# Top-32 attention and an MLP-mixer on one core: when casts, weights and the first transpositions are issued, and a new table of priorities

## The chip, the cores and the metric

The kernel runs on one core of one Trainium2 chip. Its engines run at the same time, each through its own list of instructions in order: TensorE (PE in the profile: matmuls and transpositions), VectorE (DVE), ScalarE (ACT), GpSimd (POOL) and SyncE (SP, which here only issues DMAs). The metric is device microseconds of one launch; the time before is the median of three runs, 937.52 us (936.66 to 938.66).

## The reference

Inputs are q, k and v of shape (8 batches, 8 heads, 576 rows, 64 columns) in float32, and four weights. For each batch and head:

```
scores = (q @ k.T) / 8                      # 576 x 576
kth    = 32nd largest score of each row
p      = exp(scores - rowmax) where scores >= kth, else 0
attn   = (p / sum(p)) @ v                   # 576 x 64
```

The heads of a batch are laid side by side as x (576 x 512), and the mixer computes

```
u   = x + (relu(x.T @ w_tok1) @ w_tok2).T   # w_tok1 576x256, w_tok2 256x576
out = u + relu(u @ w_ch1) @ w_ch2           # w_ch1 512x1536, w_ch2 1536x512
```

The output is (8, 576, 512) in float32.

## The kernel before, in words

**Pairs.** The unit of work is a pair of heads of one batch: 32 pairs (`u` = 0 to 31), four to a batch. Each pair's rows make nine tiles of 128 rows by 576 scores, in two groups: group 0 has four tiles, group 1 five. One pair goes through these steps:

1. SyncE loads q and k of the pair (`load_one`, L276: three DMAs each, the third for the 64 last rows; lines L289 and L292), and v from a bfloat16 copy in DRAM, `v16`. That copy is made a batch at a time by casting DMAs that GpSimd issues (`vconv`, L297). The buffers for q, k, the scores of each group and the transposed q and k are double.
2. TensorE transposes q and k (`qk_tr` L303, `qk_tail_tr` L319) and ScalarE copies the results out of PSUM (L317, L330).
3. TensorE computes the scores (`s1_mm` L337, `s0_mm` L360, `st_mm` L379), ScalarE copies them to SBUF (L350, L370, L390). Three PSUM banks, `s0`, hold scores.
4. For each group VectorE finds each row's 32nd largest score. `upper` (L401) takes the larger of the two halves of each row; `split4` (L428, L432) halves further; four rounds of MAX8 and MATCH_REPLACE8 (L445, L448) draw the largest values from these lists. Meanwhile GpSimd makes the list of the smaller halves (`both_bits` L408, `lower_bits` L416: "the list pass"), which VectorE reads in `low_round` (L461); `combine` (L466) gives the bound.
5. ScalarE makes the exponentials (L508). Five of nine tiles ("turned") are masked before that by ScalarE (`steep`, L526) and GpSimd (`sink`, L534, after `raise_kth`, L520) and then transposed by a DMA that SyncE issues (`turn`, L539). The other four are masked by ScalarE (`below_act`, L550), and transposed on TensorE (L556, L559) with ScalarE copying out (L579).
6. TensorE multiplies by v (`o_mm`, L624), VectorE inverts the denominators (`o_den`, L636), ScalarE scales (`o_ev`, L646); then the token half of the mixer for these 128 channels (`h1_mm` L666, `ut_mm` L687).

After a batch's fourth pair comes the channel half: `h2_mm` (L717, ScalarE L730) and `out_mm` (L746, ScalarE L754). For the last batch this is split: partial sums over three quarters of the channels (`pre_mm`, L1039) are made while pair 31 is in work, and `rest_mm`, `join`, `begin` and `accum` (L1103, L1115, L1081, L1094) close it.

**What sets the order.** The program is not written in the order in which it runs. Each step is added to a `Plan` as a task with an engine, an assumed duration, a priority, the tasks that it depends on and the buffers that it takes and frees. `Plan.order` (L58) then walks through assumed time: whenever an engine is free, it takes, among the tasks whose dependencies have ended and whose buffers are free, the one of the smallest priority. The result is one fixed list per engine, which on the chip runs in order, each instruction waiting for what it needs. A priority is 100 times the pair's number plus a constant of the kind of step, from the table `RANK` (L18): so a difference of 100 between two kinds is one pair. The smallest goes first. In the planner's idle time of TensorE `spare` (L261) puts in matmuls that compute nothing that is used.

Two of the planner's due times matter below. A DMA is a task without an engine (`DQ`), with a slack: a load of v waits until 12 us of assumed time after the cast of its batch is issued. And q's and k's transposition is assumed to be ready 1.3 us after the load was issued and SyncE's lag of 1.2 us.

**At the start** GpSimd issues, after the constants, in priority order: w_tok1 and w_tok2 (30), the cast of v of batch 0 (40), that of batch 1 (100 * 4 - 350 = 50), w_ch1 in two halves (210, 211), w_ch2 in two halves (220, 221), and the casts of batches 2 to 7 (450 and on). A cast depends on nothing but the cast before it.

Of the kernel before, what the change touches and what calls it, by code (L numbers as in the profile page):

```python
# [17 lines left out]
RANK = {  # L18
    "pre_mm": 21, "pre_ev": 49, "rest_mm": -29, "begin": 196, "flags": 11, "rush": 10, "rush6": -93, "load": -300,
    "qk_tr": -163, "qk_ev": -49, "s_mm": -158, "s_ev": -434, "st_mm": -106, "st_ev": -297, "keep": -185, "exp_u": 105,  # L20
    "steep": 63, "sink": 111, "exp_t": 88, "below": 404, "p_tr": -318, "p_ev": -292, "pt_tr": 92, "pt_ev": 68,
    "o_mm": 134, "o_ev": -231, "h1_mm": -373, "h1_ev": -445, "ut_mm": -358, "ut_ev": 1, "out_mm": 272, "out_ev": 225,
    "h2_mm": -3, "h2_ev": 1,
}
# [116 lines left out]
def kernel(  # L141
# [11 lines left out]
    nc = tc.nc  # L153
# [16 lines left out]
    SP = NS * P  # L170
# [12 lines left out]
    NPAIR = H // 2  # L183
# [92 lines left out]
    def load_one(st, name, src, b, p):  # L276
        if name == "v":
            src = v16
            st["vb"] = take("vb", vbufs)
            t = st["vb"][:, :, :, 0:D]  # L280
# [7 lines left out]
        for hh in range(2):  # L288
            nc.sync.dma_start(  # L289
                out=t[:, 0:NT, hh, :], in_=rws[hh, 0:W, :].rearrange("(t p) c -> p t c", p=P)  # L290
            )
        nc.sync.dma_start(  # L292
# [479 lines left out]
    add = pl.add  # L772

    def plan_weights():
        tasks = {}

        def piece(names, moves, prio):
# [9 lines left out]
            a = add("POOL", 1.2 * len(moves), prio, ld)  # L787
            x = add("DQ", 0.0, 0, lambda: None, deps=[a], slack=10.0)
# [20 lines left out]
    conv = {}  # L809
    wt = plan_weights()  # L810
    later = []
    chain = {}
# [3 lines left out]
    def plan_unit(u):  # L816
# [6 lines left out]
        if p == 0:  # L823
            conv[b] = add("POOL", 1.0, U - 350 if b else 40, lambda: vconv(b), deps=[conv.get(b - 1)])
            conv[b, "in"] = add("DQ", 0.0, 0, lambda: None, deps=[conv[b]], slack=12.0)
        for name, src in (("q", q), ("k", k), ("v", v)):
            ld[name] = add("SP", 1.75, U + RANK["load"], lambda name=name, src=src: load_one(st, name, src, b, p),
                           deps=[conv[b, "in"]] if name == "v" else [],
                           acq=[("vb" if name == "v" else "ld" + name, u)])
        vc = add("DQ", 0.0, 0, lambda: None, deps=[ld["v"]], slack=1.3)  # L830
        ev, prev = [], None
        for i in range(2):
            a = add("PE", 0.61, U + RANK["qk_tr"], lambda i=i: qk_tr(st, i), deps=[ld["qk"[i]], prev], acq=[("tp", u, "q", i)] + ([] if i else [("qkT", u)]), slack=1.3)
# [15 lines left out]
        for g in range(2):  # L849
# [35 lines left out]
            nms[g] = chain["bits"] = lob  # L885
# [395 lines left out]
```

## Time and profile before

| | |
|---|---|
| median of 3 runs | 937.52 us (936.66 to 938.66) |
| profiled execution, device time | 937.98 us |
| its span, first to last instruction | 936.1 us |
| granted TensorE clock, mean | 0.978 |
| PE, DVE, ACT, POOL busy | 856.1, 855.4, 843.7, 667.2 us |

The profiled execution lasted 1.9 us longer than its span, and is 0.46 us above the median. PE's busy time holds the spare matmuls too.

How to read it: the views give microseconds from the first instruction. A row of the timeline has the start, the duration, the engine, the line of the kernel, the operation, the tiles written and read, and how many instructions were merged; in brackets stands how long the engine had been idle before, and what ended that. "SPq" is SyncE's queue, whose rows are DMA issues; "PEld" is TensorE's weight load. In a table of windows each engine has its busy time in that stretch and, in brackets, its instructions. "q0" is the queue of GpSimd's DMAs, "q1" that of the DMAs that SyncE issues.

### The profile page before, as it was taken

How to read it: one execution, taken by the hardware profiler on the slowest of the kernel's cores; microseconds unless marked ns; L12 is line 12 of the kernel's file. 1: busy time of each engine (PE TensorE's matmuls, PEld its weight loads, DVE VectorE, ACT ScalarE, POOL GpSimd, SP SyncE). 2: the span in 40 equal slices, each digit the busy share in tenths (PEclk: the TensorE clock that was granted, in tenths of full speed). 3: DMA queues.
4: the chain of work that ended last, by engine and by line, in shares of the span. 5: the costliest groups of instructions: out<-in, count | busy, mean ns of one | idle time of the engine just before them, and what ended most of it. 6: DMA issues, size and time to landing. Idle time of an engine off the chain costs nothing.

```text
span 936.1 us, 22100 instructions
## 1 busy us (share of the span) xinstructions
PE 856.1 (91%) x7095; PEld 470.6 (50%) x7204; DVE 855.4 (91%) x3983; ACT 843.7 (90%) x1994; POOL 667.2 (71%) x510
## 2 busy tenths in 40 slices
PE   3479999999999999999999999999999999999895
PEld 3244555555554555545554555555554555555542
DVE  1495999999999999999999999999999999999942
ACT  1248999999999999999999999999999999999862
POOL 4258588777877778777787777877788778778700
PEclk8779999999999999999999999999999999999998
DMA  9962322233333334324332324323332334222201
GB/s 176 212 128 55 65 62 61 42 71 81 82 61 68 68 82 91 68 40 91 76 72 61 80 77 91 61 43 87 80 71 58 79 82 66 32 43 70 52 3 54
DMA packets 230124, 68.90 MB, mean 74 GB/s; under 512 B 222256, under 2 KB 224624, under 8 KB 229744
## 3 DMA queue, kind: packets, MB, share of 16 engines
q1 hardware_dynamic: 226624, 58.96, 29.8%
q0 software_dynamic: 3376, 8.46, 4.7%
q8 instruction: 58, 0.95, 0.4%
q14 instruction: 66, 0.54, 0.2%
HBM read 40.50 MB, written 14.16 MB: 58 GB/s over the span
## 4 chain that ended last, share of the span: by engine, by line
ACT 42%; PE 29%; DVE 19%; DMA 4%; issue 3%; SPq 3%; ACTq 0%; another core or an unknown queue 0%; DVEq 0%
ACT SS L370 6%; DVE A L445 6%; PE s L360 6%; ACT pb L508 5%; ACT U L550 5%; DVE hx L448 5%; ACT xb L646 4%; ACT E L508 4%; ACT U L526 4%; PE mps L717 4%; DMA qL<-in_q_dram 3%; ACT pt L579 3%; PE mps L265 3%; ACT H2T L730 3%; PE mps L746 2%
## 5 line engine op out<-in xcount | busy, mean ns | idle before, releaser
L408 POOL TENSOR_TENSOR lo<-SS 128x1152 int32<-128x1152 int32 x64 | 168.6, 2634 | 161.6 <-DVE A L445 134.1
L445 DVE MAX8 A<-hx 128x8 f32<-128x72 f32 (+2 forms) x1152 | 263.9, 293 | 0.0
L534 POOL TENSOR_TENSOR SS<-SS,U 128x576 f32<-128x576 f32 x158 | 198.5, 1283 | 10.8 <-ACT U L526 10.8
L448 DVE MATCH_REPLACE8 hx<-A,hx 128x72 f32<-128x72 f32 (+1 forms) x864 | 199.4, 242 | 0.0
L416 POOL TENSOR_TENSOR lo<-lo,hi 128x1152 int32<-128x1152 int32 x64 | 168.7, 2636 | 0.0
L360 PE MATMUL s<-qkT 64*128 64x512 f32 x512 | 156.2, 653 | 0.0
L370 ACT COPY SS<-s 128x512 f32<-128x512 f32 x256 | 141.6, 620 | 14.9 <-PE s L360 14.7
L401 DVE TENSOR_TENSOR hi<-SS 128x1152 f32<-128x1152 f32 x64 | 99.7, 1558 | 32.6 <-ACT SS L370 32.6
L508 ACT ACTIVATE pb<-SS,nmax 128x576 bf16<-128x576 f32 x158 | 124.9, 812 | 2.8 <-POOL SS L534 2.7
L526 ACT ACTIVATE U<-SS,kbig 128x576 bf16<-128x576 f32 x158 | 124.7, 813 | 0.9 <-POOL kbig L520 0.9
L520 POOL TENSOR_SCALAR kbig<-A 128x4 f32<-128x4 f32 (+1 forms) x63 | 101.5, 1611 | 30.1 <-DVE A L466 27.7
L461 DVE MAX8 A<-lo 128x8 f32<-128x288 f32 x256 | 100.1, 442 | 5.9 <-POOL lo L416 5.9
L717 PE MATMUL mps<-UT,wc1b 128*128 128x64 bf16 (+1 forms) x645 | 99.2, 282 | 6.4 <-ACT H2T L730 4.3
L556 PE MATMUL tp<-identB,E 128*128 128x128 bf16 (+1 forms) x650 | 101.4, 222 | 3.9 <-ACT pt L579 2.2
L559 PE MATMUL tp<-identN,U 128*128 128x128 bf16 (+1 forms) x650 | 95.8, 220 | 9.9 <-ACT U L550 8.7
L746 PE MATMUL mps<-wc2b,H2T 128*128 128x512 bf16 (+1 forms) x412 | 102.2, 380 | 1.3 <-issue 1.3
L508 ACT ACTIVATE E<-SS,nmax 128x576 bf16<-128x576 f32 x130 | 100.4, 805 | 0.2 <-POOL nmax L494 0.2
L550 ACT ACTIVATE U<-SS,A 128x576 bf16<-128x576 f32 x125 | 99.8, 821 | 0.0
L265 PEld LDWEIGHTS <-identB 128*128 128x128 bf16 x726 | 60.8, 101 | 59.1 <-issue 8.1
L717 PEld LDWEIGHTS <-wc1b 128*128 128x128 bf16 x672 | 46.4, 97 | 71.9 <-issue 37.4
L556 PEld LDWEIGHTS <-E 128*128 128x128 bf16 (+1 forms) x650 | 63.7, 100 | 35.7 <-issue 23.2
L559 PEld LDWEIGHTS <-U 128*128 128x128 bf16 (+1 forms) x650 | 62.9, 100 | 35.1 <-ACT U L550 27.1
(113 smaller groups left out, 1612.2 us busy)
## 6 DMA issues: line engine op xcount, KB each, us to landing
qL<-in_q_dram SPq DMA_DIRECT2D x64, 128.0 KB, 2.5
kL<-in_k_dram SPq DMA_DIRECT2D x64, 128.0 KB, 2.6
out_dram<-ob SPq DMA_DIRECT2D x28, 256.0 KB, 2.3
v<-in_v_dram POOLq DMA_DIRECT2D x8, 576.0 KB, 28.8
vb<-v SPq DMA_DIRECT2D x64, 64.0 KB, 2.3
pt<-pb SPq DMA_TRANSPOSE x158, 2.4
wc1b<-in_moe_w_ch_dram POOLq DMA_DIRECT2D x2, 768.0 KB, 16.8
wc2b<-in_moe_w_ch_dram POOLq DMA_DIRECT2D x2, 768.0 KB, 25.3
```

The lines of the kernel that those rows point to most:

```text
L360: nc.tensor.matmul(out=x[:, :], lhsT=T[rows[hh], 0, t * P : (t + 1) * P], rhs=T[rows[hh], 1, 0:W], start=True, stop=True,)
L370: nc.scalar.copy(out=st["SS", t // 2][:, 2 * (t % 2) + hh, 0:W], in_=st["s0", t][hh][:, :])
L408: nc.gpsimd.tensor_tensor(out=x[:, 0:4, :].bitcast(i32), in0=SS[:, 0:4, 0:HALF].bitcast(i32), in1=SS[:, 0:4, HALF:S].bitcast(i32), op=ALU.add,
L416: nc.gpsimd.tensor_tensor(out=x, in0=x, in1=st["hi"][:, 0:4, :].bitcast(i32), op=ALU.subtract)
L445: nc.vector.max(A[:, i, at], hx[:, i, 0:w])
L448: nc.vector.match_replace(hx[:, i, 0:w], A[:, i, TOP[r] : TOP[r] + 8], hx[:, i, 0:w], NEG)
L508: nc.scalar.activation(out=x, in_=srow(st, i), func=AF.Exp, bias=st["nmax", g][:, a : a + 1], scale=scale,)
L526: nc.scalar.activation(out=U[:, :], in_=srow(st, i), func=AF.Relu, bias=st["kbig", g][:, a : a + 1], scale=-STEEP,)
L534: nc.gpsimd.tensor_tensor(out=x, in0=x, in1=st["U", i][:, :], op=ALU.subtract)
L556: nc.tensor.matmul(out=out, lhsT=st["E", i][:, cols], rhs=identB[:, :], start=True, stop=False)
L559: nc.tensor.matmul(out=out, lhsT=st["U", i][:, cols], rhs=identN[:, :], start=False, stop=True)
L717: nc.tensor.matmul(out=ps[:, 0 : hi - lo], lhsT=wc1b[:, cc, fc * P : (fc + 1) * P], rhs=mst["UT"][:, cc, lo:hi], start=(cc == 0), stop=(cc ...
```

## The change

Five things are done; the values of the first are all in the diff.

- `RANK`, the table of priorities, has new values for all 34 kinds. They reach from -2256 to +2324, where they reached from -445 to +404.
- The cast of a batch's v (`conv`) depends now, for batches 1 to 7, on GpSimd's list pass of group 0 of the second pair of the batch before (`lobs[u - 3, 0]`). Its assumed slack is 18 us instead of 12.
- The cast of batch 0 and the weights are held (`held`): the cast of batch 0 and w_tok1 with w_tok2 until the list pass of pair 0's group 0, both halves of w_ch1 until that of its group 1, and one half of w_ch2 each until those of pair 1's two groups.
- k of pair 0 is loaded by ScalarE's queue instead of SyncE's.
- The transpositions of q and k of pairs 1, 2 and 3 depend now on the last score matmul of the pair before (`chain["first"]`).

```diff
 RANK = {
-    "pre_mm": 21, "pre_ev": 49, "rest_mm": -29, "begin": 196, "flags": 11, "rush": 10, "rush6": -93, "load": -300,
-    "qk_tr": -163, "qk_ev": -49, "s_mm": -158, "s_ev": -434, "st_mm": -106, "st_ev": -297, "keep": -185, "exp_u": 105,
-    "steep": 63, "sink": 111, "exp_t": 88, "below": 404, "p_tr": -318, "p_ev": -292, "pt_tr": 92, "pt_ev": 68,
-    "o_mm": 134, "o_ev": -231, "h1_mm": -373, "h1_ev": -445, "ut_mm": -358, "ut_ev": 1, "out_mm": 272, "out_ev": 225,
-    "h2_mm": -3, "h2_ev": 1,
+    "pre_mm": -619, "pre_ev": -763, "rest_mm": 23, "begin": 2294, "flags": 2033, "rush": -1060, "rush6": -1432, "load": -1622,
+    "qk_tr": 925, "qk_ev": 319, "s_mm": -2256, "s_ev": 861, "st_mm": -827, "st_ev": -1306, "keep": -1462, "exp_u": -1655,
+    "steep": -1178, "sink": 343, "exp_t": 592, "below": 2324, "p_tr": -1113, "p_ev": 1133, "pt_tr": 284, "pt_ev": 680,
+    "o_mm": -541, "o_ev": -678, "h1_mm": -281, "h1_ev": -760, "ut_mm": -245, "ut_ev": -1638, "out_mm": 1654, "out_ev": 724,
+    "h2_mm": 2300, "h2_ev": -1055,
 }
...
-    def load_one(st, name, src, b, p):
+    def load_one(st, name, src, b, p, queue=None):
+        queue = queue or nc.sync
...
-            nc.sync.dma_start(
+            queue.dma_start(
...
             a = add("POOL", 1.2 * len(moves), prio, ld)
+            held.append(a)
...
+    held = []
     wt = plan_weights()
+    lobs = {}
...
-            conv[b] = add("POOL", 1.0, U - 350 if b else 40, lambda: vconv(b), deps=[conv.get(b - 1)])
-            conv[b, "in"] = add("DQ", 0.0, 0, lambda: None, deps=[conv[b]], slack=12.0)
+            conv[b] = add("POOL", 1.0, U - 350 if b else 40, lambda: vconv(b), deps=[conv.get(b - 1), lobs.get((u - NPAIR + 1, 0))])
+            if b == 0:
+                held.insert(0, conv[b])
+            conv[b, "in"] = add("DQ", 0.0, 0, lambda: None, deps=[conv[b]], slack=18.0)
         for name, src in (("q", q), ("k", k), ("v", v)):
-            ld[name] = add("SP", 1.75, U + RANK["load"], lambda name=name, src=src: load_one(st, name, src, b, p),
+            aside = u == 0 and name == "k"
+            ld[name] = add("ACT" if aside else "SP", 1.75, U + RANK["load"],
+                           lambda name=name, src=src, aside=aside: load_one(st, name, src, b, p, nc.scalar if aside else None),
...
-            a = add("PE", 0.61, U + RANK["qk_tr"], lambda i=i: qk_tr(st, i), deps=[ld["qk"[i]], prev], acq=[("tp", u, "q", i)] + ([] if i else [("qkT", u)]), slack=1.3)
+            a = add("PE", 0.61, U + RANK["qk_tr"], lambda i=i: qk_tr(st, i), deps=[ld["qk"[i]], prev] + chain.get("first", []), acq=[("tp", u, "q", i)] + ([] if i else [("qkT", u)]), slack=1.3)
...
-            nms[g] = chain["bits"] = lob
+            nms[g] = chain["bits"] = lobs[u, g] = lob
+            if u < 2:
+                for t in held[: 2 if u == 0 else 1]:
+                    pl.after(t, lob)
+                    held.remove(t)
+            chain["first"] = smm[-1:] if u < 3 else []
```

More of the change, by code (lines that the diff above doesn't have):

```diff
@@ L288, in load_one @@
         for hh in range(2):
-            nc.sync.dma_start(
+            queue.dma_start(
                 out=t[:, 0:NT, hh, :], in_=rws[hh, 0:W, :].rearrange("(t p) c -> p t c", p=P)
             )
-        nc.sync.dma_start(
+        queue.dma_start(
             out=t[0:TAIL, NT, :, :], in_=rws[:, W:S, :].rearrange("h p c -> p h c")
```

## The prediction

> **What bounds the kernel now.** I read the page first, then a table of windows cut where VectorE's first pass over a pair's lists begins, then the timeline of the first 42 us and of the stretch from 62 to 99 us. The page: three engines are busy for about 90% of the span, so shares alone say nothing. The row of q0 is GpSimd's DMA queue, the last two rows are what the change moves.
>
> ```profile
> span 936.1 us, 22100 instructions
> PE 856.1 (91%) x7095; PEld 470.6 (50%) x7204; DVE 855.4 (91%) x3983; ACT 843.7 (90%) x1994; POOL 667.2 (71%) x510
> ...
> q0 software_dynamic: 3376, 8.46, 4.7%
> ...
> v<-in_v_dram POOLq DMA_DIRECT2D x8, 576.0 KB, 28.8
> wc1b<-in_moe_w_ch_dram POOLq DMA_DIRECT2D x2, 768.0 KB, 16.8
> ```
>
> The windows are: up to VectorE's first list pass, pair 0, pair 1, pairs 2 to 4, 5 to 23, 24 to 30, VectorE's part of pair 31, and the end.
>
> ```profile
> core 0: us, PE busy (x) PEld busy (x) DVE busy (x) ACT busy (x) POOL busy (x), PEclk, DMA share, GB/s
> 0.00:36.30 36.30, 16.07 (x132) 12.08 (x132) 2.70 (x9) 6.37 (x13) 11.64 (x33) 0.72 1.04 187
> 36.30:62.20 25.90, 13.63 (x91) 7.88 (x90) 25.83 (x122) 8.32 (x22) 15.43 (x8) 0.74 0.84 174
> 62.20:99.30 37.10, 35.43 (x256) 17.87 (x261) 26.77 (x125) 30.99 (x63) 22.85 (x18) 1.00 0.25 57
> 99.30:177.80 78.50, 74.89 (x608) 40.78 (x617) 78.40 (x371) 73.22 (x167) 60.53 (x45) 1.00 0.33 64
> 177.80:672.80 495.00, 474.88 (x4008) 261.55 (x4070) 494.62 (x2338) 492.06 (x1181) 383.27 (x285) 1.00 0.34 72
> 672.80:857.10 184.30, 176.62 (x1468) 96.38 (x1490) 182.18 (x862) 182.79 (x439) 149.91 (x105) 1.00 0.30 60
> 857.10:886.10 29.00, 26.02 (x260) 15.82 (x262) 26.52 (x128) 26.20 (x62) 23.10 (x15) 1.00 0.22 62
> 886.10:930.00 43.90, 38.55 (x283) 18.27 (x288) 18.37 (x41) 23.70 (x55) 0.43 (x1) 1.00 0.12 35
> ```
>
> From pair 2 on VectorE is the bound: pairs 5 to 23 take 495.0 us, 26.05 each, and it works 494.62 of them. ScalarE stands right behind it with 492.06. What is not bound work is at the start (VectorE works 2.70 of 36.3 us), in pair 1 (26.77 of 37.10, so 10.3 idle) and in the end of 43.9 us, where TensorE is busy for 38.55.
>
> **Part 1, the start.** The order on TensorE and what it waited for:
>
> ```profile
> 3.83 5.51 PE L265 MATMUL O<-identB 128*128 128x128 bf16 x60 [3.83 <-DVE O L255]
> ...
> 9.18 0.61 PE L307 MATMUL tp<-identF,qL 128*128 128x128 f32 x4
> ...
> 9.62 1.06 PE L265 MATMUL O<-identB 128*128 128x128 bf16 x16
> ...
> 10.52 0.61 PE L307 MATMUL tp<-identF,kL 128*128 128x128 f32 x4
> ...
> 11.97 0.66 PE L337 MATMUL s<-qkT 64*128 64x64 f32 x8
> ...
> 23.23 1.09 PE L307 MATMUL tp<-identF,qL 128*128 128x128 f32 x4 [10.60 <-DMA qL<-in_q_dram]
> ...
> 32.10 1.09 PE L307 MATMUL tp<-identF,kL 128*128 128x128 f32 x4 [5.78 <-DMA kL<-in_k_dram]
> ...
> 33.12 2.08 PE L360 MATMUL s<-qkT 64*128 64x512 f32 x4
> ...
> 35.23 1.07 ACT L370 COPY SS<-s 128x512 f32<-128x512 f32 x2 [1.42 <-PE s L360]
> ...
> 35.67 0.85 PE L337 MATMUL s<-qkT 64*128 64x64 f32 x8
> ...
> 36.34 1.36 DVE L401 TENSOR_TENSOR hi<-SS 128x1152 f32<-128x1152 f32 x1 [32.56 <-ACT SS L370]
> ...
> 39.55 1.07 ACT L370 COPY SS<-s 128x512 f32<-128x512 f32 x2 [0.54 <-PE s L360]
> ```
>
> Pair 0 is transposed by about 11.1 us and its first scores are made at 11.97. Then pair 1's q stands next in TensorE's list and has not landed: 10.60 us of waiting; after half of pair 0's scores comes pair 1's k: 5.78 more. So VectorE starts at 36.34. The loads are late because all casts and weights were issued ahead of them or among them; the row of SyncE's loads (L289) shows the best, the median and the worst time to land:
>
> ```profile
> DMA to landing us min/median/max: 2.0/2.5/30.2
> ```
>
> The change takes both causes away: with pair 1's transpositions behind pair 0's last scores, TensorE's list can't meet a late load in between, whatever the DMAs do. The new start step by step. q of pair 0 keeps its 60 spare matmuls, since its assumed due time (1.75 + 1.2 + 1.3 = 4.25 us) is unchanged: 9.18. k is now assumed ready at 1.75 + 0.15 + 1.3 = 3.2, before q's transposition has ended, so the 16 spares between them go: 10.52 - (9.18 + 0.61) = 0.73 us earlier, first scores at 11.24. From there to the last score copy of a group costs what it cost for group 1 of this pair: 35.67 to 39.55 + 1.07 = 40.62, so 4.95, and 0.04 to VectorE: 16.2. That is **20.1 us** earlier. The dearer price would be two halves as at 33.12 to 35.23 + 1.07, 3.18 each, behind 0.66: 7.0, a start at 18.3 and 18.0 us. I take 4.95, the same steps with no late load among them. Three DMA issues on ScalarE's queue cost nothing: it has nothing to copy before q is transposed at 9.18.
>
> **Part 2, pair 1.** VectorE's two long waits there, and what stood before the first of them:
>
> ```profile
> 67.27 2.11 ACT L526 ACTIVATE U<-SS,kbig 128x576 bf16<-128x576 f32 x3
> ...
> 68.13 3.76 POOL L534 TENSOR_TENSOR SS<-SS,U 128x576 f32<-128x576 f32 x3 [10.07 <-ACT U L526]
> ...
> 77.73 1.18 DVE L461 MAX8 A<-lo 128x8 f32<-128x288 f32 x3 [5.93 <-POOL lo L416]
> ...
> 92.33 0.20 DVE L636 RECIPROCAL rden<-O 128x5 f32<-128x5 f32 x1 [4.21 <-PE O L624]
> ```
>
> GpSimd waited 10.07 us for pair 0's masks, which ScalarE made only at 67.27, behind the copies of the next pairs' late scores; so pair 1's list pass was late, and VectorE lost 5.93 us. The 4.21 at 92.33 are the first product with v, late by the same chain. In the new order no cast leaves before the first list pass is over. That pass ended 9.1 us after VectorE's start before (the row of L416 below: 42.85 + 2.60 = 45.45, against 36.34), so now at about 25.3; pairs 1 and 2 are loaded before that, at 2.5 us each. I take the 5.93 as gone. For the second wait I leave 2 us: casts and weights now run beside pairs 0 and 1. The queue's 4.7% are 44.0 us of all engines for 8.46 MB, 5.2 us a MB, so both halves of w_ch1 (1.57 MB) fill them for 8.2 us, in which a transposing DMA or v's load for the first product can be late. Ends: all 10.3 us come back, or a whole burst of 8.2 stays and 2.1 come back. **8.3 us.** ScalarE's part fits: its 30.99 us of pair 1 exceed 26.1 by 4.9, and it idles for 17.6 in pair 0 and 5.3 in pairs 2 to 4.
>
> **Part 3, GpSimd's issues among the list passes.**
>
> ```profile
> 5.20 1.06 POOL L298 DMA_DIRECT2D v<-in_v_dram  x2
> 6.21 1.50 POOL L781 DMA_DIRECT2D wc1b<-in_moe_w_ch_dram  x2
> ...
> 42.85 2.60 POOL L416 TENSOR_TENSOR lo<-lo,hi 128x1152 int32<-128x1152 int32 x1
> ...
> 45.90 1.16 DVE L461 MAX8 A<-lo 128x8 f32<-128x288 f32 x3
> ...
> 47.94 4.44 POOL L520 TENSOR_SCALAR kbig<-A 128x4 f32<-128x4 f32 x1 [2.49 <-DVE A L466]
> ```
>
> An issue takes 0.5 to 0.8 us, and GpSimd is free for (495.0 - 383.27) / 19 = 5.9 us per pair: I cost them at nothing. If an issue is held as the small product at 47.94 was, whose 4.44 us lie beside VectorE's next list pass, and stands right ahead of a list pass, VectorE loses all but the 0.45 us between 45.45 and 45.90: 4.0 us at each of ten places (four held, six later casts). The casts of batches 1 to 7 themselves need 0.59 x 5.2 = 3.1 us of the DMA engines per batch of 104: nothing, and they come more than a pair ahead of their use.
>
> The page "SBUF — State Buffer" of the Trainium skill, in "SBUF: two separate sides", warns that a DMA issued by GpSimd gets no descriptors while VectorE holds the shared ports in a two-port mode; in "Who interferes with whom" it exempts tensor_tensor, which takes the read side only. By the warning the sum would be up to 40 us higher, by the exemption it stays; no row of before has an issue beside a list pass.
>
> **Part 4, the table.** Between pairs 5 and 23 the new order can gain no more than VectorE's idle 0.4 us; behind them 2.1 in pairs 24 to 30 and 2.5 in pair 31. It can lose what it makes ScalarE idle: that has 495.0 - 492.06 = 2.9 us for 19 pairs, 0.15 each. I take 0. Score copies (+861) now go behind the masks and exponentials of the same pair (-1178, 592), but still ahead of the copies of transposed tiles (1133) and of `below` (2324), and the scores' buffers are double: they have a pair's time, 26 us, to be ready in. In the end TensorE's work of 38.55 us stays. The last batch's steps go ahead by ten pairs ("rush"), batch 6's `h2_mm` goes back by nine (2300 - 1432); TensorE had 3 us idle in pair 31 to take partial sums early, so -3, or as much late, +3; I take 0.
>
> **Sum.** 937.98 - 20.1 - 8.3 = 909.6, forecast **910 us** (the profiled execution is 0.46 above the median, which I leave).
>
> **The rivals.**
>
> *Given back in the ramp.* The start is won, but the casts now fall among the first lists: 918 if pair 1's 10.3 us stay, 926 with a burst of 8.2 on top. For it: loads took up to 30.2 us beside that queue. Against: bursts of 8 us now, not one of 44. The page "DMA: Bandwidth & Descriptors" of the skill has each DMA engine take turns between queues packet by packet ("Queues, rings and completion order"). By it a load of 512 rows, 32 turns an engine at 44.0 x 16 / 3376 = 0.21 us, passes a burst in some 7 us, an estimate, and this rival would end near 922.
>
> *Slower: ScalarE waits in the new order.* Place: the copies of scores, which can stand ahead of the matmuls that feed them, as in this row of the waits (total, times, longest):
>
> ```profile
> ACT SS L370 <- PE s L360: 14.7, 15, 3.1
> ```
>
> A wait is 0.98 us on average. ScalarE has 0.15 us a pair to lose, so one more wait in each of the 27 pairs from 5 on costs 26 us (936), two 53 (963). It decides from 28.4 / 27 = 1.05 us a pair. For it: every priority is new, and ScalarE has no room. Against: the double buffers, and no such wait bound VectorE in 19 pairs.
>
> *Slower: GpSimd caught.* Part 3's 4.0 us at all ten places, 950; it decides from seven.
>
> *No earlier start.* k on ScalarE's queue lands late, or another wait takes the first one's place on TensorE: 930 (pair 1's gain alone) to 938. Against: k's 10.52 was not waited for even beside the weights.
>
> *Better still.* All 10.3 us, 3 of the end and the 4.6 of pairs 24 to 31: 900.
>
> **How the numbers follow.** Forecast (903 to 917) 0.58, ramp 0.16, ScalarE's waits 0.07, GpSimd caught 0.03, no earlier start 0.04, better still 0.12. The runs of before spread by 0.2%, so 2 us either way count as the same. Faster: 0.58 + 0.16 + 0.12 + 0.03 of "no earlier start" = 0.89; same 0.01; slower 0.07 + 0.03 = 0.10. The range 899 to 927 holds the forecast, nearly all of the ramp's case and two thirds of the better one: 0.81.
>
> **What would show it.** Part 1: VectorE's first L401 near 16 us (18 at most), no DMA wait at L307 between the first and last scores of pair 0. Part 2: VectorE's idle time in pair 1 at 2 us, the first L636 with a wait under 3. Part 3: no wait of L461 for L416 above a us, casts spread one to a batch. Part 4: 26.0 to 26.1 us per pair, and about 44 us from VectorE's last bound to the last store. The prediction is wrong if pairs take over 26.5 us, or if the start is early and the first ten pairs idle it away.

## The result and the profile after

The changed kernel takes 942.41 us (median of 13 runs, 938.92 to 943.69) against 937.49 us (13 runs of the kernel before, on the same chips): a ratio of 1.0042, 95% interval 1.0031 to 1.0053. It is slightly slower, by 0.4%; the forecast was 910. The profiled execution lasted 941.98 us, with a span of 940.1. Lines 278 to 789 of the changed kernel have numbers one higher than before's (L401 is now L402, L624 is L625, L636 is L637).

The page of the kernel after, its span, busy times and GpSimd's DMA queue:

```profile
span 940.1 us, 22219 instructions
...
PE 868.0 (92%) x7209; PEld 467.6 (50%) x7209; DVE 862.9 (92%) x3983; ACT 849.2 (90%) x1994; POOL 691.7 (74%) x510
...
q0 software_dynamic: 3376, 8.46, 5.8%
```

VectorE has 7.5 us more of busy time for the same 3983 instructions. The windows of the kernel after are cut as those of before were as far as the start of pair 31: the start, pair 0, pair 1, pairs 2 to 4, 5 to 23, 24 to 30. The last two are VectorE's part of pair 31 and the end, and they can't be set beside before's row by row: before's cut at 886.10 is where VectorE has pair 31's last bound, which is at 889.0 here, and before's last row stops 6.1 us short of the end of its span.

```profile
0.00:15.50 15.50, 11.43 (x122) 9.23 (x122) 2.70 (x9) 5.14 (x10) 2.27 (x18) 1.00 0.58 115
15.50:41.30 25.80, 23.03 (x164) 12.02 (x163) 25.76 (x122) 15.31 (x33) 21.84 (x16) 0.87 0.51 86
41.30:82.40 41.10, 33.47 (x226) 17.71 (x224) 28.88 (x126) 25.90 (x53) 24.64 (x20) 0.92 0.97 128
82.40:161.00 78.60, 73.72 (x583) 39.40 (x581) 78.53 (x370) 71.77 (x165) 59.27 (x44) 1.00 0.29 60
161.00:669.30 508.30, 480.64 (x4068) 259.77 (x4066) 498.43 (x2339) 496.04 (x1181) 409.32 (x290) 1.00 0.38 78
669.30:857.70 188.40, 178.26 (x1508) 95.31 (x1508) 183.71 (x863) 184.66 (x440) 150.89 (x106) 1.00 0.30 61
857.70:896.20 38.50, 34.63 (x331) 20.03 (x327) 33.49 (x140) 33.17 (x79) 23.52 (x16) 0.96 0.23 60
896.20:940.00 43.80, 32.84 (x220) 14.14 (x219) 11.37 (x28) 17.20 (x39) 0.00 (x0) 0.94 0.09 29
```

Set against the windows of before, taken between the starts of VectorE's `upper` to a hundredth: the start is 20.84 us shorter, pair 0 the same (-0.06), pair 1 is 3.95 longer, pairs 2 to 4 are 0.11 longer, pairs 5 to 30 are 17.39 longer (696.76 against 679.37), and pair 31 with the end is 3.39 longer (31.3 us to the last bound and 51.1 from there, against 28.9 and 50.0). The sum is +3.9, the difference of the spans. So the 20.8 us won at the start are real, and they are paid back: 17.4 us at 0.67 us a pair from pair 5 on, the rest in pair 1 and at the end. In pairs 5 to 23 (508.30 against 495.0) VectorE now stands idle for 508.30 - 498.43 = 9.9 us, where it stood for 0.4, and works 3.8 us longer (498.43 - 494.62).

The start, from the timeline of the kernel after:

```profile
8.52 0.61 PE L308 MATMUL tp<-identF,qL 128*128 128x128 f32 x4
...
10.62 0.66 PE L338 MATMUL s<-qkT 64*128 64x64 f32 x8
...
15.50 1.36 DVE L402 TENSOR_TENSOR hi<-SS 128x1152 f32<-128x1152 f32 x1 [11.72 <-ACT SS L371]
...
19.92 0.66 PE L308 MATMUL tp<-identF,qL 128*128 128x128 f32 x4
```

Pair 1's q is transposed at 19.92, behind all of pair 0's scores, and nothing there waits for a DMA. Pair 1 is where the ramp loses its gain again:

```profile
66.37 1.09 PE L308 MATMUL tp<-identF,qL 128*128 128x128 f32 x4 [6.02 <-DMA qL<-in_q_dram]
...
72.33 1.05 PE L625 MATMUL O<-vb,pt 128*128 128x65 bf16 x25
...
73.42 0.20 DVE L637 RECIPROCAL rden<-O 128x5 f32<-128x5 f32 x1 [10.08 <-PE O L625]
...
82.25 0.20 DVE L637 RECIPROCAL rden<-O 128x5 f32<-128x5 f32 x1 [2.10 <-PE O L625]
```

VectorE no longer waits for GpSimd's list pass there, as it did for 5.93 us before. But the wait for the first product with v has grown from 4.21 to 10.08, and a second one of 2.10 follows. In TensorE's list pair 3's q stands ahead of that product, and TensorE waits 6.02 us for it to land.

The same pair of producer and consumer is what changed in the steady pairs. These are rows of VectorE's waits between 160 and 860 us (total us, times, longest us), of the kernel before:

```profile
DVE rden L636 <- PE O L624: 1.0, 2, 0.6
```

and of the kernel after:

```profile
DVE rden L637 <- PE O L625: 12.3, 23, 1.3
```

VectorE reaches the inversion of the denominators, in the middle of its list of selections, before TensorE has made the product. No wait is longer than 1.3 us, so no single late instruction stands out in the page; only the waits by name and stretch show it.

### The profile page after: what moved, and what is told of

It reads as the page before. It is cut to its first block, busy times and chain, and to the rows that moved or that the text cites. A ratio compares the mean times of both kernels' runs of the same rounds, so it can differ in the third digit from the quotient of the medians.

```text
span 940.1 us, 22219 instructions
## 1 busy us (share of the span) xinstructions
PE 868.0 (92%) x7209; PEld 467.6 (50%) x7209; DVE 862.9 (92%) x3983; ACT 849.2 (90%) x1994; POOL 691.7 (74%) x510
## 4 chain that ended last, share of the span: by engine, by line
ACT 41%; PE 40%; DVE 8%; POOL 5%; DMA 3%; issue 2%; SPq 0%; ACTq 0%; DVEq 0%
PE mps L747 9%; PE s L361 7%; ACT U L527 6%; ACT SS L371 6%; ACT pb L509 5%; ACT H2T L731 4%; PE O L625 4%; ACT E L509 4%; ACT U L551 3%; ACT xb L647 3%; POOL kbig L521 3%; ACT pt L580 3%; PE O L265 3%; PE mps L265 2%; PE tp L557 2%
## 5 line engine op out<-in xcount | busy, mean ns | idle before, releaser
L446 DVE MAX8 A<-hx 128x8 f32<-128x72 f32 (+2 forms) x1152 | 267.4, 308 | 0.0
L371 ACT COPY SS<-s 128x512 f32<-128x512 f32 x256 | 146.5, 607 | 22.3 <-PE s L361 22.3
L521 POOL TENSOR_SCALAR kbig<-A 128x4 f32<-128x4 f32 (+1 forms) x63 | 124.4, 1974 | 43.6 <-DVE A L467 42.3
L361 PE MATMUL s<-qkT 64*128 64x512 f32 x512 | 150.7, 643 | 2.5 <-ACT SS L371 2.5
L527 ACT ACTIVATE U<-SS,kbig 128x576 bf16<-128x576 f32 x158 | 115.3, 804 | 11.1 <-POOL kbig L521 11.1
L402 DVE TENSOR_TENSOR hi<-SS 128x1152 f32<-128x1152 f32 x64 | 102.8, 1606 | 11.7 <-ACT SS L371 11.7
L718 PE MATMUL mps<-UT,wc1b 128*128 128x512 bf16 (+1 forms) x672 | 100.6, 286 | 12.7 <-ACT H2T L731 10.7
L747 PE MATMUL mps<-wc2b,H2T 128*128 128x512 bf16 (+1 forms) x420 | 105.1, 380 | 0.0
L509 ACT ACTIVATE E<-SS,nmax 128x576 bf16<-128x576 f32 x130 | 96.4, 796 | 0.2 <-POOL nmax L495 0.2
L449 DVE MATCH_VALUE_LOAD hx<-A,hx 128x8 f32 x864 | 80.1, 93 | 0.0
```

The source lines that it names most:

```text
L361: nc.tensor.matmul(out=x[:, :], lhsT=T[rows[hh], 0, t * P : (t + 1) * P], rhs=T[rows[hh], 1, 0:W], start=True, stop=True,)
L371: nc.scalar.copy(out=st["SS", t // 2][:, 2 * (t % 2) + hh, 0:W], in_=st["s0", t][hh][:, :])
L446: nc.vector.max(A[:, i, at], hx[:, i, 0:w])
L449: nc.vector.match_replace(hx[:, i, 0:w], A[:, i, TOP[r] : TOP[r] + 8], hx[:, i, 0:w], NEG)
L509: nc.scalar.activation(out=x, in_=srow(st, i), func=AF.Exp, bias=st["nmax", g][:, a : a + 1], scale=scale,)
L527: nc.scalar.activation(out=U[:, :], in_=srow(st, i), func=AF.Relu, bias=st["kbig", g][:, a : a + 1], scale=-STEEP,)
```

## The experiments

Each kernel differs from the kernel after (names beginning with a_) or from the kernel before (b_) by the edit shown; bc_ and o_ start from another experiment. "Order kept" means that the planner sees the same tasks and writes the same lists, and that only what a task issues is moved. The lengths in the table are distances between starts of VectorE's `upper` in each kernel's profiled execution, in us; the last column but one is the mean of pairs 5 to 30. For a_oldrank that execution is the fastest of four, which spread from 973.49 to 987.82 us; the others lie within 3 us of their medians.

| kernel | median | start | pair 1 | pairs 2-4 | a pair, 5-30 | pair 31 and end |
|---|---|---|---|---|---|---|
| before | 937.49 | 36.3 | 37.1 | 78.5 | 26.13 | 79.0 |
| after | 942.41 | 15.5 | 41.1 | 78.6 | 26.80 | 82.3 |
| a_ksync | 942.40 | 15.4 | 40.7 | 78.7 | 26.89 | 80.5 |
| a_dmafirst | 933.00 | 15.8 | 36.4 | 78.6 | 26.69 | 81.2 |
| a_burstlate | 941.76 | 16.3 | 37.8 | 81.0 | 26.84 | 81.0 |
| a_lightout | 936.65 | 15.6 | 40.8 | 78.7 | 26.65 | 81.9 |
| a_oldrank | 981.52 | 16.8 | 35.4 | 92.6 | 27.88 | 76.3 |
| o_nofirst | 967.69 | 16.3 | 39.2 | 78.5 | 27.94 | 77.1 |
| b_newrank | 958.19 | 37.6 | 35.5 | 79.2 | 26.67 | 83.5 |
| b_conv | 976.53 | 33.3 | 30.9 | 78.5 | 28.08 | 75.7 |
| b_first | 940.92 | 17.1 | 39.9 | 92.6 | 26.11 | 78.5 |
| b_castlate | 924.58 | 34.1 | 26.2 | 78.5 | 26.14 | 78.4 |
| b_dmalate | 911.06 | 17.3 | 27.2 | 79.7 | 26.17 | 79.0 |
| a_kbig_dve | 934.38 | 16.8 | 38.3 | 79.1 | 26.63 | 79.1 |
| bc_kbig_dve | 934.68 | 35.6 | 27.1 | 79.3 | 26.53 | 75.8 |
| b_kbig_dve | 942.46 | 36.8 | 36.7 | 79.3 | 26.36 | 76.3 |

### The table and the dependencies apart

The first question was whether the new table or the new dependencies make the pairs longer. a_oldrank takes the table of before into the changed kernel, b_newrank the new table into the kernel before.

```diff
-RANK = { ... the values of one kernel ... }
+RANK = { ... the values of the other ... }
```

> The changed kernel with the old table of priorities. If the table costs the time of pairs 5 to 30 (696.8 us against 679.4) and of the end (3.4 us), those come back: pairs of 26.1 us, VectorE's start still at 15.5 us, and 919 to 923 us in all if pair 1 keeps its 12 us of idle VectorE. If instead the casts spread over the batches make the pairs longer, pairs stay at 26.7 us and the time at 938 to 942.

> The kernel before with the new table alone. If the table makes the pairs longer: VectorE starts near 36 us as before, pairs 5 to 30 take about 696 us, and the time is 954 to 962. If the spread casts do it: 936 to 941.

a_oldrank took 981.52 us, ratio 1.0481 (1.0445 to 1.0518); b_newrank 958.19, ratio 1.0215 (1.0198 to 1.0232). Neither half is harmless. On the dependencies of before the new table costs 20.7 us; with the new dependencies it saves 981.52 - 942.41 = 39 us (31 by a_oldrank's fastest run). The table cannot be called good or bad by itself: it fits one set of dependencies.

The dependencies were then tried one at a time in the kernel before, without the table: b_conv has only the casts' wait for a list pass, b_first only the transpositions' wait for the scores. o_nofirst is a_oldrank without the latter.

```diff
 # b_conv
-            conv[b] = add("POOL", ..., deps=[conv.get(b - 1)])
+            conv[b] = add("POOL", ..., deps=[conv.get(b - 1), lobs.get((u - NPAIR + 1, 0))])
 # b_first; o_nofirst takes the first of these two lines back
-            a = add("PE", 0.61, U + RANK["qk_tr"], ..., deps=[ld["qk"[i]], prev], ...
+            a = add("PE", 0.61, U + RANK["qk_tr"], ..., deps=[ld["qk"[i]], prev] + chain.get("first", []), ...
+            chain["first"] = smm[-1:] if u < 3 else []
```

> The kernel before with one edit of the change alone, and a new order made from it: a batch's cast depends on the list pass of the second pair of the batch before. The casts are then tasks of GpSimd among the list passes. If such a task in the order, not its DMA, is what lengthens the pairs, pairs 5 to 30 go from 26.1 to 26.5 or more (a_oldrank: 27.9) although VectorE starts earlier, and the time is 925 to 960. If pairs stay at 26.1, the time is near b_castlate's 924.6.

> The kernel before with one edit of the change alone: pairs 1 to 3 are transposed behind the last scores of the pair before. If TensorE's wait for late loads is what holds pair 0 back, VectorE starts at 16 to 18 us beside the same crowd of casts (20 us won), and what comes later shows what the edit does to the order: the 14 us that pairs 2 to 4 lost in a_oldrank appear here too if it is this edit that costs them. By both: 928 to 936; with no cost in the order: 916 to 922.

> a_oldrank without that one edit (the changed kernel, the old table, pairs 1 to 3 transposed as early as they can be). If the edit made pairs 2 and 4 last 33 us, pairs 2 to 4 fall from 92.6 to 78 to 80 us and the time from 981 to 965 to 970; pairs 5 to 23 stay near 27.9. If the casts in the order did that, pairs 2 to 4 stay.

b_conv took 976.53 us, ratio 1.0398 (1.0370 to 1.0426). This one line, seven DMAs issued later, makes pairs 5 to 30 longer by 730.1 - 679.4 = 50.7 us, and the same row of VectorE's waits between 160 and 860 us says where:

```profile
DVE rden L636 <- PE O L624: 50.6, 23, 5.2
```

b_first took 940.92, ratio 1.0028 (1.0017 to 1.0040): its start is nearly as early as the change's, 17.1 us, and the gain is lost in pairs 0 to 4 (pair 0 grows from 25.8 to 31.4, pair 1 by 2.8, pairs 2 to 4 by 14.0, in which VectorE is idle for 14.0), while pairs 5 to 30 stay at 26.11. o_nofirst, 967.69 and 1.0329 (1.0301 to 1.0357), confirms both: without "first", pairs 2 to 4 are back at 78.5, and the 27.94 of the later pairs stay.

### The DMAs alone, in the order of before

If an order, and not the late DMAs, costs the time, then issuing the DMAs late without telling the planner should bring the gain. In b_castlate only the casts of batches 1 to 7 are moved: the planner's tasks remain but issue nothing, and each cast is issued right behind a list pass. In b_dmalate the cast of batch 0, the weights and, behind that cast, the loads of v of the first three pairs are moved as well. The places are not quite the change's own: w_ch2 goes behind pair 2's list passes instead of pair 1's, and the casts behind the pass of group 1 instead of group 0.

```diff
+    def bits_then(st, u, g):
+        lower_bits(st, g)
+        if (u, g) == (0, 0):            # b_dmalate only
+            vconv(0); parts[0](); [f() for f in vfirst]
+        if (u, g) == (0, 1):            # b_dmalate only
+            parts[1](); parts[2]()
+        if u == 2:                      # b_dmalate only
+            parts[3 + g]()
+        if u % NPAIR == 1 and g == 1 and u // NPAIR + 1 < B:
+            vconv(u // NPAIR + 1)
```

> The kernel before, order kept; only the casts of batches 1 to 7 are moved, each behind the list pass of the second pair of the batch before; the weights and the cast of batch 0 stay at the start. They take some 22 us of the DMA engines where all took 44. If the crowd as a whole made pair 1's q and k late, VectorE starts at 20 to 27 us instead of 36 and the time is 920 to 929. If the weights alone are enough to hold the loads back, it stays at 33 to 36 and 935 to 938.

> The kernel before with its table and with the order of its four computing engines kept; only GpSimd's DMAs are moved: the cast of batch 0 and w_tok1, w_tok2 behind the list pass of pair 0's group 0, w_ch1 behind group 1's, w_ch2 behind those of pair 2, the cast of each later batch behind the list pass of the second pair of the batch before; the loads of v of pairs 0 to 2 stand behind the first cast. If the change's gain is in the DMAs and its loss in the new order, VectorE starts at 16 to 18 us and pairs 5 to 30 stay at 26.1 (679 to 682 us), with 909 to 920 in all, 909 if pair 1's wait goes too. If DMAs among the lists make the pairs longer, pairs are 26.5 and more and the time 925 to 937.

b_castlate took 924.58 us, ratio 0.9861 (0.9846 to 0.9876): pair 1 is 11.0 us shorter, the start only 2.3. b_dmalate took **911.06 us** (910.23 to 912.21, five runs), ratio 0.9719 (0.9706 to 0.9733). It beats both kernels, and its windows up to pair 30 can be held against the prediction's parts:

```profile
0.00:17.30 17.30, 13.44 (x132) 11.38 (x132) 2.73 (x10) 6.35 (x14) 2.26 (x18) 1.00 0.46 103
17.30:43.10 25.80, 25.33 (x175) 13.68 (x175) 25.77 (x122) 17.74 (x39) 21.94 (x17) 1.00 0.65 113
43.10:70.30 27.20, 26.32 (x188) 12.76 (x187) 27.17 (x126) 22.36 (x45) 21.81 (x17) 1.00 0.68 133
70.30:150.00 79.70, 74.60 (x606) 40.60 (x605) 79.60 (x371) 72.89 (x166) 62.38 (x48) 1.00 0.46 83
150.00:645.60 495.60, 480.93 (x4070) 261.50 (x4069) 495.05 (x2337) 492.45 (x1181) 388.96 (x290) 1.00 0.37 78
645.60:830.30 184.70, 179.05 (x1492) 96.52 (x1491) 182.32 (x862) 183.20 (x440) 150.58 (x106) 1.00 0.31 63
```

Pairs 5 to 23 take 495.6, as before, and pairs 5 to 30 are 1.0 us longer. So late casts at these places cost next to nothing. The start is early here with the transpositions where they were, and in b_first with the DMAs where they were: to take away either of the two causes that the prediction names is enough. In b_conv the casts are issued behind list passes too, and 50 us are lost: that loss is not in the DMAs but in the lists that the planner writes once it knows of the dependency (bc_kbig_dve below gets 40 of them back in these pairs, with the casts left where b_conv has them).

### Pair 1

Two theories stood for pair 1's 41.1 us: a burst of DMAs (a cast and half of w_ch2 are issued at 51.6 to 53.2 us), in which pair 3's q took about 10 us to land, or the order. a_dmafirst keeps the order and issues the weights and the casts of batches 0 and 1 first; it leaves the other casts out and takes v from the two batches that are there. a_burstlate keeps the order and moves only the halves of w_ch2 behind pair 2's list passes. a_c2late lets the planner do that. a_ksync puts k of pair 0 back on SyncE's queue.

```diff
 # a_dmafirst, ahead of the first instruction of the list
+        early[0](); vconv(0); vconv(1)
+        for ld in early[1:]: ld()
 # a_burstlate, behind lower_bits
+        if u == 2: moved[g]()
 # a_c2late
-            if u < 2:
+            if u in (0, 2):
 # a_ksync
-   ... load_one(st, name, src, b, p, nc.scalar if aside else None),
+   ... load_one(st, name, src, b, p),
```

> The changed kernel with every engine's order kept, but GpSimd issues the weights and the casts of batches 0 and 1 before everything else; the casts of batches 2 to 7 are left out (their pairs read v of batch 0 or 1). If the order alone makes the pairs longer, pairs 5 to 30 stay at 26.7 to 26.8 us; if the spread casts do, they go to 26.1 (18 us less). If pair 1's 12 us of idle VectorE come from the burst at 51 to 66 us, they fall under 4; pair 0 starts later, at 15.5 to 20, as its loads then meet the weights. By the order: 930 to 940; by the casts: 912 to 920.

> The changed kernel with every engine's order kept; only the two halves of w_ch2 are issued behind the list passes of pair 2 instead of pair 1. If the burst makes pair 3's q and k late and with them pair 0's product with v, the wait of 10.1 us falls to 2 to 4 and the time by 5 to 9, to 933 to 937. If TensorE's order alone does it, the time stays within 2 us.

> The changed kernel with the two halves of w_ch2 held until the list passes of pair 2 instead of pair 1. If the burst of w_ch2 behind the cast of batch 1 is what made pair 3's q and k land 7 to 10 us after their issue and VectorE wait 10.1 us for pair 0's product with v, that wait falls under 4 us and the time by 6 to 9, to 933 to 936. If the order on TensorE alone makes that product late, the wait stays and the time is within 2 us of 942.

> The changed kernel with every order kept, but k of pair 0 issued on SyncE's queue behind q. If the issue time on SyncE's queue counts, VectorE starts 1 to 2 us later than 15.5 and the time grows by as much; if TensorE's 60 spare matmuls (to 8.5 us) cover the landing, the start stays within 0.3 us and the time within 1 us.

a_dmafirst took 933.00 us, ratio 0.9941 (0.9924 to 0.9958). Its pair 1 is 4.7 us shorter than after's, and it still has both waits:

```profile
68.41 0.20 DVE L637 RECIPROCAL rden<-O 128x5 f32<-128x5 f32 x1 [6.38 <-PE O L625]
...
77.90 0.20 DVE L637 RECIPROCAL rden<-O 128x5 f32<-128x5 f32 x1 [2.76 <-PE O L625]
```

Without the burst the waits are 9.1 us instead of 12.2. How much of the 12.2 is the burst's and how much the order's does not follow from that, since other things changed with it: TensorE no longer waits for pair 3's q, and its granted clock in pair 1 is 1.00 instead of 0.92, but GpSimd's small product `kbig`, which comes up again below, takes 4.45 us in a_dmafirst, where it took 1.51 in the kernel after (at 54.56).

```profile
54.30 4.45 POOL L521 TENSOR_SCALAR kbig<-A 128x4 f32<-128x4 f32 x1 [1.07 <-DVE A L467]
```

The run answers another question plainly: with every order kept and no late cast, pairs 5 to 30 still take 26.69 us each. What makes them long is for the most part the order. a_burstlate (941.76, ratio 1.0034, 1.0013 to 1.0055) took 3.3 us out of pair 1 and lost 2.4 again in pairs 2 to 4, where the moved weights then ran; its TensorE still waits 3.46 us for pair 3's q beside the cast alone. a_c2late gave 969.98 us, ratio 1.0334 (1.0317 to 1.0352): pair 1 is down to 30.6, but pairs 2 to 4 take 108.7 and the later ones 27.13. A planned move of two DMAs changed the lists so much that the run says nothing on the burst, which is why a_burstlate keeps the order. a_ksync took 942.40, ratio 1.0047 (1.0030 to 1.0063), start 15.44: the queue of k makes no difference.

### What is late first in the longer pairs

The product with v is late; three guesses as to why. a_slack8 makes the planner place VectorE's inverse of the denominators 8 us of assumed time behind the product with v instead of 3. a_lightout takes work off TensorE: it leaves out part of the channel half's second product. a_nospare takes away the spare matmuls after the first 30 us.

```diff
 # a_slack8
-RSLACK = 3.0
+RSLACK = 8.0
 # a_lightout, in out_mm
+            if 3 <= x < n - 1 and x % 3:
+                continue
 # a_nospare, in spare
+        if at > SETTLED:
+            return
```

> The changed kernel with VectorE's inverse of the denominators placed 8 us of assumed time behind the product with v instead of 3 (RSLACK; the last batch keeps its 0.3). If the longer pairs are VectorE standing in its list at that inverse (12.3 us in pairs 5 to 30), most of that goes: 26.1 to 26.3 us per pair in batches 2 to 5, 930 to 936 in all. If TensorE is the bound in these pairs, the wait moves elsewhere and the time stays within 3 us.

> The changed kernel with every order kept and 7 of 15 matmuls of each tile of out_mm left out (the output lacks their terms), about 2 us of TensorE's work per pair. If TensorE, full with the channel half in some pairs, makes the products with v late and VectorE wait, the 12.3 us of waits in pairs 5 to 30 fall under 4 and the time by 8 to 14, to 928 to 934. If the products are late for the order of ScalarE's and SyncE's steps before them, the waits stay above 9 and the time within 4 us of 942.

> The changed kernel without the spare matmuls after 30 us of assumed time. If spare matmuls standing in TensorE's list ahead of the product with v make it late, the waits of VectorE at the denominators (32 us in all) fall by half and pairs go to 26.1 to 26.4, 925 to 933 in all. If TensorE's own work fills the pairs, nothing is won, and a lower granted clock in the gaps may lengthen the pairs: 942 to 960.

a_slack8 took 953.23 us, ratio 1.0161 (1.0144 to 1.0178): VectorE's idle time in pairs 5 to 23 halves (from 9.87 to 4.53), but these pairs take 507.6 against 508.3, and pair 31 with the end takes 96.1. The waits for the product between 160 and 860 us fall from 12.3 to 3.4 us there, and nothing is won by it: VectorE works for 503.0 us in pairs 5 to 23 instead of 498.4. Its own list operations are held now: `split4`'s first one takes up to 1.99 us beside GpSimd's `sink`, where its longest was 0.90 before. a_lightout took 936.65, ratio 0.9988 (0.9968 to 1.0009); the waits for the product between 160 and 860 us are still 10.8 us of 12.3. A full TensorE is at most a small part of the cause, though the 5.8 us that the time fell by are more than the second of the two forecasts allowed and less than the first asked for. a_nospare took 977.82, ratio 1.0423 (1.0403 to 1.0442), and tests another thing, the granted clock:

```profile
core 0: 976.5 us, clock 0.867
```

With the spares the kernel after has 0.988; at the lower clock the waits for the product grow to 41.0 us. The spare matmuls are needed. Whether they also delay the product this run can't say, since the clock fell with them.

The traces then gave a candidate. In the longer pairs GpSimd's small product `kbig` (L521), from which ScalarE makes the masks of the turned tiles, misses the gap between two of VectorE's list operations. Rows of the kernel after:

```profile
360.17 0.39 DVE L467 MAX8 A<-A 128x8 f32<-128x16 f32 x4
360.48 1.64 DVE L402 TENSOR_TENSOR hi<-SS 128x1440 f32<-128x1440 f32 x1
360.65 4.45 POOL L521 TENSOR_SCALAR kbig<-A 128x4 f32<-128x4 f32 x1 [0.47 <-DVE A L467]
362.03 0.46 DVE L425 TENSOR_TENSOR low<-SS 128x288 f32<-128x288 f32 x1
...
364.04 0.97 DVE L433 TENSOR_TENSOR hx<-lo 128x360 f32<-128x360 f32 x2
...
365.13 2.11 ACT L527 ACTIVATE U<-SS,kbig 128x576 bf16<-128x576 f32 x3 [0.62 <-POOL kbig L521]
```

An instruction whose shortest run is 0.23 us, and whose median is 1.51, takes 4.45, until VectorE's two-input operations are over at 364.04 + 0.97 = 365.01; ScalarE's mask follows at once. The page "SBUF — State Buffer" of the Trainium skill, in "Who interferes with whom", says that a VectorE instruction with two SBUF inputs contends with a GpSimd instruction that reads SBUF; the trace agrees, and shows it held through a whole run of such instructions. Rows of more than 4 us number 5 of 63 before, 13 after and 14 in b_conv; in the kernel after they come every 53 us, in a rhythm with the waits. This is a coincidence in time, so it was tested: `kbig` is made by VectorE, at the end of `combine`, in the order of the kernel after (a_kbig_dve), of b_conv (bc_kbig_dve), and, as a control, of the kernel before (b_kbig_dve). GpSimd's task stays in the plan and issues nothing, so each order is kept.

```diff
     def combine(st, g):
...
+        x = m8p.tile([P, NS], f32, name="kbig", tag="kbig")
+        n = 4 + g
+        nc.vector.tensor_scalar_mul(x[:, 0:n], A[:, 0:n, KTH + 7], STEEP)
+        st["kbig", g] = x
```

> The changed kernel in its own order, with the small product kbig made by VectorE at the end of its combine step instead of by GpSimd; nothing else moves. Theory K (what is late first is that small product, held on GpSimd through VectorE's next list passes, with the masks, exponentials, transpositions and the product with v behind it): VectorE's waits at rden for TensorE's O between 160 and 860 us, 12.3 us in the changed kernel, fall under 4 us. VectorE pays for 63 more instructions; by its reciprocal of 128x5 (0.20 us) at most 12.6 us, at half of that 6.3, so the time comes out between 935 and 946. Rival N (the small product is held because it is late anyway, or has slack; the order of ScalarE's and TensorE's own lists makes O late): the waits stay at 9 to 13 us, and the time is 946 to 956.

> The kernel before with the casts' dependency alone (976.53 us, waits at rden for O of 50.6 us between 160 and 860 us), and kbig made by VectorE as in the run beside it. Theory K: the waits fall to under 15 us and the time to 940 to 955. Rival N: the waits stay above 40 us, and the time is 976 to 990.

> The kernel before, with kbig made by VectorE and nothing else: the control of the two runs before it, in an order where the product with v is not late (1.0 us of waits at rden for O between 160 and 860 us). If the gain of 42 us in the order with the casts' dependency came from the wait that the held product sets off, this kernel has nothing to win by it and pays for VectorE's 64 instructions, 18 us with the gaps (0.25 us each and 2.2 of idle time): 945 to 956, pairs 5 to 23 at 26.4 to 26.6. If the move is a gain whatever the order, it is faster than 937.5.

bc_kbig_dve took 934.68 us, ratio to before 0.9969 (0.9956 to 0.9981): 41.9 us less than b_conv. Over the whole run its waits for the product, 50.6 us in b_conv's steady pairs alone, are

```profile
DVE rden L640 <- PE O L628: 1.3, 1, 1.3
```

a_kbig_dve took 934.38, ratio 0.9958 (0.9938 to 0.9979), and its waits between 160 and 860 us fell from 12.3 us to

```profile
DVE rden L641 <- PE O L629: 1.9, 3, 1.0
```

The control took 942.46, ratio 1.0048 (1.0031 to 1.0064): 4.7 us slower than the kernel before, since VectorE pays for 64 more instructions (0.19 us each there, 0.25 and 0.26 in the other two) and between 160 and 860 us there was only 1.0 us of waits to cure. So the wait for the product is set off by `kbig` on GpSimd and by what stands behind it in GpSimd's list. Which of these two it is, the masks that wait for `kbig` itself or the work held up behind it, was not told apart.

How much of the longer pairs that explains can be counted. In pairs 5 to 30 the move takes 696.8 - 692.3 = 4.5 us out of the order of the kernel after and adds 685.3 - 679.4 = 5.9 to that of the kernel before. If the move costs VectorE the same 5.9 in both, 10.4 of the 17.4 us between the two orders go with `kbig`, and 7.0 stay.

A second piece works the other way round, and it comes from the casts. In the kernel after a cast stands between the list pass of group 0 and the `sink` behind it. The issue takes 0.59 to 0.62 us and moves `sink` back by as much, into VectorE's next `upper`. Rows of the kernel after, and of a_dmafirst, which has the same order without the cast:

```profile
384.48 0.59 POOL L299 DMA_DIRECT2D v<-in_v_dram  x1
385.09 2.52 POOL L535 TENSOR_TENSOR SS<-SS,U 128x576 f32<-128x576 f32 x2
386.83 2.31 DVE L402 TENSOR_TENSOR hi<-SS 128x1440 f32<-128x1440 f32 x1
...
377.50 2.54 POOL L535 TENSOR_TENSOR SS<-SS,U 128x576 f32<-128x576 f32 x2
379.87 1.68 DVE L402 TENSOR_TENSOR hi<-SS 128x1440 f32<-128x1440 f32 x1
```

At the casts of batches 2 to 7 this `upper` takes 2.31 to 2.46 us in the kernel after and 1.67 to 1.81 at the same places in a_dmafirst: 3.8 us in all, most of the 5.3 that VectorE works longer in pairs 5 to 30. In a_kbig_dve it is VectorE's new `kbig` that is held there, for 0.6 us at each of the six casts.

## Why the prediction was wrong

The profiled execution took 941.98 us against the sum's 909.6, 32.4 more. Part 2 is 12.2 of that (8.3 forecast, 3.95 lost), what comes behind pair 1 (Part 4) is 20.9, and Part 1 gained 0.7 more than forecast.

**Part 1 was right.** The start was to be 16.2 us and is 15.50, by the steps given: q transposed at 8.52 (9.18 forecast), first scores at 10.62 (11.24), then 4.88 to VectorE (4.95 and 0.04).

**Part 2 was right on its first wait and wrong on its second.** The wait of 5.93 us for GpSimd's list pass is gone, as said. "For the second wait I leave 2 us" failed: it is 10.08 and 2.10. The dearer end, a whole burst, still had 2.1 us come back, and 3.95 were lost. A late load was the danger that the prediction saw; that the new order puts pair 3's q ahead of the product on TensorE, which waits 6.02 us for it, it did not see. With no burst 9.1 us of waits remain (a_dmafirst), so the order around pair 1, which the prediction took as unchanged, has a part in it; the shares were not told apart. In the old order the step holds better than it was written: b_dmalate's pair 1, with w_ch2 moved on to pair 2, takes 27.2, 9.9 us less than before, where 8.3 were forecast.

**Part 3 was nearly right on the chip and incomplete in the plan.** An issue of a cast takes 0.57 to 0.62 us and no list pass waits for it. Nothing is not quite what it costs: the delayed `sink` holds VectorE's `upper`, 3.8 us at six casts, of which 696.8 - 693.9 = 2.8 us show in pairs 5 to 30 (a_dmafirst); b_dmalate, whose casts stand elsewhere, shows 1.0 (680.3 against 679.4). The exemption that the page "SBUF — State Buffer" of the Trainium skill, in "Who interferes with whom", gives to tensor_tensor is what the one issue beside such an operation in the kernel after agrees with: the cast at 26.86 takes 0.57 us beside `upper`, as it did with VectorE idle (0.57 at 5.20 before). The 40 us of the other reading did not come. What the step left out is that a cast with a dependency is another task for the planner: the order of everything is planned anew, and that alone costs 50.7 us in pairs 5 to 30 under the old table (b_conv).

**Part 4 failed: "I take 0".** Pairs 5 to 30 are 17.4 us longer and pair 31 with the end 3.4 (just outside the 3 that was allowed for the end either way). The working looked for room on ScalarE and allowed it to lose 0.15 us a pair. But the bound was on the wrong engine: the greatest part, 10.4 of the 17.4 us, goes with a small product on GpSimd that the new order lets fall beside VectorE's list operations, and GpSimd's 5.9 us of free time a pair say nothing on whether it meets a gap between them. The prediction had the row of this effect in hand, 4.44 us at 47.94 before, and used it only for DMA issues.

**The rivals.** "ScalarE waits" had the right sign, but the wrong place; the waits are VectorE's, for the product, and that its 936 lies near the 942 is luck. The longer pairs, at 0.67 us each, stayed below the 1.05 from which that rival alone decides, and a loss of the ramp's kind made up the rest: pair 1 gave nothing back and took 3.95. The prediction had counted a loss in the ramp and one in the pairs as alternatives, and they came together. "GpSimd caught" named the right engine and the right mechanism with the wrong instruction, and 4.0 us a place where the casts cost 0.6. The forecast itself, 910, is what b_dmalate takes (911.06): the sum fits the DMA part of the change, in the order of before, though in part by luck, since the start gained 19.1 where 20.1 were forecast and pair 1 9.9 where 8.3 were.

**What stays open.** Why the casts' dependency leads the planner to lists in which `kbig` is late more often was not followed further. The code has one place to look at: in assumed time every task of GpSimd, a cast's issue of 1.0 us included, shuts out VectorE's `upper` and `split4` while it runs, and they shut it out (`port`, L46 and L87 to L90). Of the 7.0 us that remain in pairs 5 to 30 of a_kbig_dve against its control, 3.8 are VectorE's `kbig` held at the six casts and 2.3 are idle time; the last 0.9 are open. So is the share of the burst in pair 1. And a_slack8 shows that taking the waits away is not enough by itself: its pairs are no shorter.

## What to carry to other kernels

Where a planner writes the instruction lists, a moved DMA is two changes: the transfer, and a new order of everything. Try them apart, by issuing the transfer from another place in an unchanged order; here late transfers in the order of before were worth -26 us (b_dmalate), and the changed kernel, with its new order, is 31 us above that. Free time of an engine is no room for a small instruction that must run at one moment; look for the longest run of a short instruction, and for who waits behind it. It can go either way: an issue of 0.6 us on one engine can move its next instruction into the way of the other.

## What was not expected of the hardware

- A GpSimd tensor_scalar on 128x4 or 128x5 elements took 0.23 us at the least, 1.51 at the median and up to 4.45 beside VectorE's two-input tensor_tensor operations; moving these 64 instructions to VectorE was worth 42 us in one order, 8 in a second, and cost 5 in a third.
- In the other direction VectorE's tensor_tensor on 128x1440 elements, 1.65 us at the median, took up to 2.46 beside GpSimd's tensor_tensor of `sink`.
- Taking away the spare matmuls after the first 30 us lowered the granted clock from 0.988 to 0.867 and cost 977.82 - 942.41 = 35 us.
- 128 KB loads of q and k, which land in 2.6 us at the median, took 7 to 10 us beside a cast and half of w_ch2 (9.7 and 8.1 for pair 3's q and k in the kernel after).
